# Gram and triangle products spread over eight tiles of the array, the triangle applied to the Gram side

## Chip, cores and metric

The kernel runs on one core of a Trainium2 chip. The metric is the device time of one execution in microseconds (us).

## What is computed

The input is a delta-rule attention over 4 batches of 8 heads, 768 positions and a head size of 48, followed by two feed-forward layers over the 3072 tokens. All inputs and outputs are float32 (the weights are wider on arrival and are decoded in the kernel). Cut to what matters:

```python
k_n = k / (np.linalg.norm(k, axis=-1, keepdims=True) + 1e-06)
state = np.zeros((B, H, D, D), dtype=np.float32)
for t in range(S):
    kt, vt, bt = (k_n[:, :, t], v[:, :, t], beta[:, :, t, None])
    y[:, :, t] = np.einsum('bhd,bhde->bhe', q[:, :, t], state)
    v_old = np.einsum('bhde,bhd->bhe', state, kt)
    state = state + bt[:, :, :, None] * np.einsum('bhd,bhe->bhde', kt, vt - v_old)
x = y.transpose(0, 2, 1, 3).reshape(B * S, H * D)
x = (silu(x @ w_gate) * (x @ w_val)) @ w_out      # 384 -> 1536 -> 384
out = elu(x @ w_in) @ w_out2                      # 384 -> 2048 -> 384
```

## The kernel before, in words

**Groups.** The recurrence is done in blocks of 32 positions. One group is 128 positions of 2 batches: 16 units (8 heads for each of the two batches, a = 0 and 1), each with C = 4 blocks of 32 positions, which lie at the partitions 0, 32, 64 and 96. There are 12 groups. A unit has the number u = 8 a + 2 j + par.

**Work of one group.** `loads` fetches k and q into `kp` and `qp`, and v into the right half of `R`. `prepare` normalises the keys, copies them into the left half of `R` (`rk`, L425, on ACT), writes beta times key into `gr` (`kb`, L430, on POOL), transposes keys and queries into `kq` (L441), and multiplies the blocks' keys with keys and queries (`gram`, L467: 32 rows of output, 64 columns, contraction over 48). `mask` (L473, on DVE) writes the strictly triangular parts of that, times beta, into `gr`. `invert` computes the inverse of the unit triangular 32x32 block of each unit on DVE: transposes into `ain` (L502), 31 elimination steps of a product and a sum (`whole`, L517 and L524), or, in groups 0, 1 and 2 (`BLOCKED`), 15 steps on the two halves at once (`halves`, L534 and L540), and a transpose back (L548); in the blocked groups a second transpose (L553) and two matmul steps (`join1`, L562, and `join2`, L576) put the halves together. The result is `zt`.

`attention` then applies the triangle: `xstep` (L618) multiplies `zt` with the 96 columns of `R`, four units to a step and four steps to a group, and `xput` (L622, on ACT) writes the result back into `R`. `gstep` (L638) multiplies `R` with the 80 columns of `gr`, and `put` (L647) evicts that into `lc`. `chain` (L671) carries the state over the blocks, `yall` (L694) makes the outputs, `xtr` (L718) transposes them for the feed-forward part.

**Feed-forward.** `moe1` (L853, L878) follows on each group: 12 times two projections of 9 matmuls and a product of 9. After the last group `moe2` (L963, L1000) runs over all tokens.

**Small matmuls.** Each step on 32 positions is a matmul that takes a part of the rows of the 128x128 array (the partitions of its operands) and a part of its columns (the partitions of its output). `gram` before uses 48 rows and four column groups, one unit parity after the other; `xstep` uses the four places on the diagonal, rows and columns 32 c. The trace has two records for each such matmul of the program, so 64 matmuls of a group are 128 records.

**Order.** The program writes its own order. Steps are handed to `Order.add` with an engine, an estimated duration, a priority, what they read and write, and how many PSUM banks they need (`Slots`; the pool AT has four). `Order.run` then lists the steps of each engine by estimated start and priority, so PE's order of attention and feed-forward work is fixed when the program is built. Where its plan has PE idle before 150 us, it puts filler matmuls (`fill`, L1030). Changed estimates change the order.

**Queues.** All loads and stores are issued on SP's queue in the planned order; the weight loads of the first feed-forward layer (L756, L759) follow the loads of group 0.

Of the kernel before, what the change touches and what calls it, by code (L numbers as in the profile page):

```python
# [17 lines left out]
ALU = mybir.AluOpType  # L18
# [162 lines left out]
def delta_moe_kernel(ctx: ExitStack, tc: tile.TileContext, q, k, v, beta,  # L181
                     wg, wv, wo, w_in, w_out, out):
    nc = tc.nc
# [9 lines left out]
    C = 4  # L193
# [175 lines left out]
    def loads(g, p, then=None):  # L369
# [12 lines left out]
    def prepare(g, p):  # L382
# [40 lines left out]
        def rk(a):  # L423
            u = slice(a * 8, a * 8 + 8)
            A.copy(out=R[:, u, 0:D], in_=kp[:, u, 0:D])  # L425
# [26 lines left out]
        for a in range(2):  # L452
            add(p, pool(384, lambda a=a: kb(a)), r=["nbt", "kp", ("kp", a)], w=[("grk", a)])
            add(p, act(384, lambda a=a: rk(a), False), r=["kp", ("kp", a)], w=[("Rk", a)])
        for a in range(2):
            l = []
            for par in range(2):
                h = Slots(AT, 1)

                def gram(a=a, par=par, h=h):  # L460
                    x = bank[h.got[0]][:, 0:256].rearrange("p (n w) -> p n w", n=4)
                    b = 64 * par
                    for j in range(4):
                        m = kq[b:b + D, a, j]
                        for c in range(C):
                            t = slice(32 * c, 32 * c + 32)
                            PE.matmul(x[t, j, :], lhsT=m[:, 1, t], rhs=m[:, :, t], start=True,  # L467
                                      stop=True, skip_group_check=True)

                def mask(a=a, par=par, h=h):  # L470
# [6 lines left out]

                def rest(a=a, par=par, h=h, mask=mask):
                    add(p, dve(256, mask), r=[h, "z"], w=[("grm", a, par)], use=[h])
                l.append((470, gram, [("kq", a, 0), ("kq", a, 1)], h, [("grm", a, par)], rest))  # L480
            batch(p, 6, l, g > 0)
# [4 lines left out]
    def invert(g, p):  # L486
# [18 lines left out]
        def whole(l):  # L505
            c0 = l // 2
            cuts = [(c0, 16)]
            if l * (16 - c0) > 40:
                cuts = [(c0, c0 + (16 - c0) // 2), (c0 + (16 - c0) // 2, 16)]
            b = 32 * (l + 1) % 1024  # L510
            ts = [ain[:, b + l * (x - c0):b + l * (y - c0)].rearrange("p (j n) -> p j n", n=y - x)
                  for x, y in cuts]
# [600 lines left out]
```

## Time and profile before

| | us |
|---|---|
| three runs | 1160.48, 1164.08, 1164.74 |
| median of the three | 1164.08 |
| profiled execution | 1164.54 |
| its span | 1162.80 |
| PE busy in the span | 1131.3 |
| DVE busy | 776.8 |
| ACT busy | 576.5 |
| POOL busy | 44.2 |

The span runs from the first to the last instruction of the program; 1.7 us of the execution lie around it. In the views, an engine is busy while one of its records runs; records of matmuls overlap, so many of them together take less time than their sum. "PEld" is the loading of weights, "xN" is a number of records, and PEclk is the share of the full TensorE clock that was granted in a stretch. "issue" as a releaser means that the profile shows nothing that the engine waited for.

### The profile page before, as it was taken

What the parts mean: (1) busy time and instruction counts of PE and PEld (TensorE: products, weight loads), DVE (VectorE), ACT (ScalarE), POOL (GpSimd) and SP (SyncE); (2) the same over time, 40 slices, a digit from 0 to 9 for tenths busy, and PEclk for the clock granted to TensorE, in tenths of its full rate; (3) what the DMA queues carried; (4) which work ended last, traced back from release to release, by engine and by line L of the source; (5) the groups of instructions that cost most, each with busy time, mean ns of one, the idle gap of its engine ahead of it and who ended that gap; (6) DMA issues with size and microseconds to landing.
All of it is one profiled execution on the core that took longest, in us unless ns stands there. A gap on an engine that the chain in (4) does not pass through costs nothing.

```text
span 1162.8 us, 34253 instructions
## 1 busy us (share of the span) xinstructions
PE 1131.3 (97%) x14766; PEld 1051.0 (90%) x14766; DVE 776.8 (67%) x2430; ACT 576.5 (50%) x1110; POOL 44.2 (4%) x61
## 2 busy tenths in 40 slices
PE   8889989999999999999999999999999999999998
PEld 7779889999999999899999999988889889888887
DVE  7789857877778786778786844996545444454444
ACT  8688433434343434243434344995545454454443
POOL 2000000000000000000000000000000000000000
PEclk9899899999999999899999999999999999999999
DMA  9650202020202020202020004900101001010000
GB/s 245 200 161 16 43 2 44 16 43 16 44 16 44 22 50 10 36 18 42 22 50 10 22 2 141 353 15 28 55 1 55 1 19 37 1 37 1 28 1 27
DMA packets 106822, 57.33 MB, mean 49 GB/s; under 512 B 76944, under 2 KB 101520, under 8 KB 106672
## 3 DMA queue, kind: packets, MB, share of 16 engines
q1 hardware_dynamic: 106672, 55.16, 17.5%
q8 instruction: 115, 1.88, 0.7%
q14 instruction: 35, 0.29, 0.1%
HBM read 45.71 MB, written 9.44 MB: 47 GB/s over the span
## 4 chain that ended last, share of the span: by engine, by line
PE 89%; DVE 5%; ACT 3%; issue 2%; DMA 0%; ACTq 0%; DVEq 0%
PE gv L853 27%; PE acc L878 12%; PE acc L1000 8%; PE at L1000 8%; PE at L963 8%; PE gv L963 8%; PE at L671 3%; PE at L638 3%; PE at L618 3%; PE at L441 2%; PE at L467 2%; PE at L694 1%; DVE z L540 1%; DVE ain L534 1%; PE at L718 1%
## 5 line engine op out<-in xcount | busy, mean ns | idle before, releaser
L853 PE MATMUL gv<-xh,w 128*128 128x256 f32 x1728 | 297.1, 291 | 1.0 <-ACT tb L860 0.9
L853 PEld LDWEIGHTS gv<-xh,w 128*128 128x128 f32 x1728 | 242.4, 193 | 9.1 <-ACT tb L860 1.4
L878 PE MATMUL acc<-hb,w 128*128 128x256 f32 x1296 | 182.3, 285 | 0.7 <-DVE hb L870 0.6
L878 PEld LDWEIGHTS acc<-hb,w 128*128 128x128 f32 x1296 | 165.9, 192 | 2.7 <-DVE hb L870 1.0
L860 ACT ACTIVATE tb<-gv 128x256 f32<-128x256 f32 x144 | 55.3, 384 | 200.3 <-PE gv L853 199.2
L853 PE MATMUL gv<-xl,w 128*128 128x256 f32 x864 | 151.7, 285 | 0.0
L853 PEld LDWEIGHTS gv<-xl,w 128*128 128x128 f32 x864 | 125.6, 194 | 0.0
L867 ACT CAST hb<-tb 128x256 fp32r<-128x256 f32 x144 | 58.5, 406 | 121.0 <-DVE tb L863 120.2
L863 DVE TENSOR_TENSOR tb<-gv,tb 128x256 f32<-128x256 f32 x144 | 60.7, 422 | 66.9 <-ACT tb L860 38.7
L978 DVE SCALAR_TENSOR_TENSOR hb<-gv,hb 128x512 f32<-128x512 f32 x48 | 33.2, 691 | 91.6 <-ACT hb L975 91.6
L524 DVE TENSOR_TENSOR z<-z,ain 128x60 f32<-128x60 f32 (+32 forms) x522 | 88.7, 209 | 0.9
L517 DVE TENSOR_TENSOR ain<-z,ain 128x60 f32<-128x60 f32 (+32 forms) x522 | 87.7, 204 | 0.6
L978 DVE SCALAR_TENSOR_TENSOR hb<-at,hb 128x512 f32<-128x512 f32 x48 | 33.1, 690 | 81.1 <-ACT hb L975 81.0
L870 DVE TENSOR_TENSOR hb<-tb,hb 128x256 fp32r<-128x256 f32 x144 | 66.3, 460 | 22.4 <-ACT hb L867 21.4
L969 ACT ACTIVATE hb<-gv 128x512 f32<-128x512 f32 x48 | 28.7, 597 | 96.7 <-PE gv L963 96.5
L975 ACT ACTIVATE hb<-hb,neg 128x512 f32<-128x512 f32 x96 | 69.5, 724 | 2.7
L969 ACT ACTIVATE hb<-at 128x512 f32<-128x512 f32 x48 | 28.7, 597 | 79.4 <-PE at L963 79.1
L972 ACT ACTIVATE hb<-hb 128x512 f32<-128x512 f32 x96 | 60.7, 633 | 2.8
L638 PE MATMUL at<-gr,R 32*96 32x80 f32 x1488 | 45.3, 251 | 0.0
L638 PEld LDWEIGHTS at<-gr,R 32*96 32x96 f32 x1488 | 37.7, 159 | 6.4
L1000 PE MATMUL acc<-w,ain 128*128 128x384 f32 x192 | 39.7, 340 | 1.8 <-DVE ain L983 1.2
L963 PE MATMUL gv<-lc,w 128*128 128x512 f32 x144 | 41.0, 394 | 0.0
(192 smaller groups left out, 2089.4 us busy)
## 6 DMA issues: line engine op xcount, KB each, us to landing
w<-in_moe_w_out_dram SPq DMA_DIRECT2D x28, 384.0 KB, 6.7
w<-in_moe_w_in_dram SPq DMA_DIRECT2D x16, 384.0 KB, 6.2
kp<-in_k_dram SPq DMA_DIRECT2D x12, 384.0 KB, 4.1
qp<-in_q_dram SPq DMA_DIRECT2D x12, 384.0 KB, 4.1
R<-in_v_dram SPq DMA_DIRECT2D x24, 192.0 KB, 2.8
w<-in_moe_w_gate_dram SPq DMA_DIRECT2D x12, 384.0 KB, 6.8
w<-in_moe_w_val_dram SPq DMA_DIRECT2D x12, 384.0 KB, 6.7
x2d<-hb SPq DMA_DIRECT2D x12, 256.0 KB, 2.0
```

What stands on the lines that cost most here:

```text
L517: V.tensor_tensor(out=t, in0=z[:, l:l + 1, x:y].to_broadcast([128, l, y - x]), in1=an[:, l, 0:l].unsqueeze(2).to_broadcast([128, l, y - x] ...
L524: V.tensor_tensor(out=z[:, 0:l, x:y], in0=z[:, 0:l, x:y], in1=t, op=ALU.add)
L638: PE.matmul(bank[h[c].got[0]][0:96, s * 80:s * 80 + 80], lhsT=R[t, u, :], rhs=gr[t, u, 0:80], start=True, stop=True, skip_group_check=True)
L853: PE.matmul(dst, lhsT=wt[:, a_, kk * 128:(kk + 1) * 128], rhs=xx[:, kk, :], start=(n == 0), stop=(n == 3 * KD - 1))
L863: V.tensor_tensor(out=c['s'], in0=bank[h.got[0]][:, TB:2 * TB], in1=c['s'], op=ALU.mult)
L870: return lambda: e.tensor_tensor(out=c['h'][:, 1, :], in0=c['s'], in1=c['h'][:, 0, :].bitcast(F32), op=ALU.subtract)
L878: PE.matmul(o_, lhsT=w[:, a_, d * 128:(d + 1) * 128], rhs=c['h'][:, b_, :], start=(f == 0 and n == 0 and d != 1), stop=(f == F1 - 1 and n ...
L963: PE.matmul(x, lhsT=W[f][:, 0, a_, kk * 128:(kk + 1) * 128], rhs=x2[n][b_][:, kk, :], start=(m == 0), stop=(m == 3 * KD - 1))
L972: A.activation(out=c['r'], in_=c['r'], func=ACTF.Exp, scale=-1.0)
L975: A.activation(out=c['r'], in_=c['r'], func=ACTF.Identity, bias=neg1, scale=1.0)
L978: V.scalar_tensor_tensor(out=c['r'], in0=bank[h.got[0]], scalar=0.0, in1=c['r'], op0=ALU.max, op1=ALU.add)
L1000: PE.matmul(o, lhsT=c['h'][:, b_, t * 128:(t + 1) * 128], rhs=W[f][:, 1][:, a_, :], start=(f == 0 and m == 0), stop=(f == F2 - 1 and m == 2))
```

## The change

**Gram.** The matmuls of both parities of one a go into one step, alternating: parity 0 uses the rows 0 to 47, parity 1 the rows 64 to 111, each with four column groups, and each parity writes its own PSUM bank. There are two Gram steps to a group in place of four.

**Triangle.** `xstep` multiplies `zt` with the 80 columns of `gr` in place of the 96 columns of `R`, and `xput` writes `gr` in place of `R`. Eight units go into one step and two banks: units 0 to 3 of an a use the diagonal, units 4 to 7 the places two column groups further. The results of the latter therefore come out shifted by two blocks of 32 positions. So that `gstep` finds both factors on the same partitions, `R` of these units is shifted in the same way: the copy of the keys and the load of v are cut into three pieces each (one for the unshifted units, one for each half of the shifted ones). `put` undoes the shift with its output pattern.

**Inversion.** As the triangle now stands on the other side, its transpose is needed: the elimination runs from the first position up in place of from the last down, with the same number and sizes of steps, reading columns of `an` in place of rows. In the blocked groups `join1` reads `zt` and `join2` reads the second transpose.

The diff, without the changed dependences of `load_x2`:

```diff
@@ loads
         for a in range(2):
-            add(p, dma(196608, lambda a=a: nc.sync.dma_start(
-                out=R[:, a * 8:a * 8 + 8, D:2 * D], in_=src_of(v, g, a, a + 1)), 160.0), w=[("Rv", a)])
+            def rv(a=a):
+                x = src_of(v, g, a, a + 1)
+                for u0, p0, p1, m0 in ((0, 0, 128, 0), (4, 0, 64, 64), (4, 64, 128, 0)):
+                    nc.sync.dma_start(out=R[p0:p1, a * 8 + u0:a * 8 + u0 + 4, D:2 * D],
+                                      in_=x[m0:m0 + p1 - p0, u0:u0 + 4])
+            add(p, [("SP", 1290.0, 0.0, 196608 / 160.0, rv)], w=[("Rv", a)])
@@ prepare
-            add(p, act(384, lambda a=a: rk(a), False), r=["kp", ("kp", a)], w=[("Rk", a)])
+            for n, c in enumerate(((0, 0, 128, 0), (4, 0, 64, 64), (4, 64, 128, 0))):
+                add(p, act(192, lambda a=a, c=c: rk(a, *c), False), r=["kp", ("kp", a)], w=[("Rk", a, n)])
         for a in range(2):
-            l = []
+            h = [Slots(AT, 1) for par in range(2)]
+
+            def gram(a=a, h=h):
+                for j in range(4):
+                    for c in range(C):
+                        for par in range(2):
+                            t = slice(32 * c, 32 * c + 32)
+                            m = kq[64 * par:64 * par + D, a, j]
+                            PE.matmul(bank[h[par].got[0]][t, 64 * j:64 * j + 64], lhsT=m[:, 1, t],
+                                      rhs=m[:, :, t], start=True, stop=True, skip_group_check=True)
+            add(p, pe(620, gram, 6), r=[("kq", a, 0), ("kq", a, 1)], w=h, need=h,
+                wait=[("grm", a, 0), ("grm", a, 1)])
...
-                l.append((470, gram, [("kq", a, 0), ("kq", a, 1)], h, [("grm", a, par)], rest))
-            batch(p, 6, l, g > 0)
@@ invert, whole
-                                    in1=an[:, l, 0:l].unsqueeze(2).to_broadcast([128, l, y - x]),
+                                    in1=an[:, l + 1:32, l:l + 1].to_broadcast([128, m, y - x]),
...
-        for l in range(15 if blocked else 31, 0, -1):
+        for l in range(15 if blocked else 31):
@@ invert, joins
-                    PE.matmul(x[r:r + 32, u], lhsT=gr[r:r + 16, u, 80:112], rhs=d1t[r:r + 16, u],
+                    PE.matmul(x[r:r + 32, u], lhsT=gr[r:r + 16, u, 80:112], rhs=zt[r:r + 16, u],
...
-                    PE.matmul(x[t, u], lhsT=buf['v'][t, u], rhs=zt[t, u], start=True, stop=True,
+                    PE.matmul(x[t, u], lhsT=d1t[t, u], rhs=buf['v'][t, u], start=True, stop=True,
...
-        add(p, pe(1250, join1, 8), r=GRM + ALLA[2:], w=[h1], need=[h1], wait=["z"])
+        add(p, pe(1250, join1, 8), r=GRM + ALLA[:2], w=[h1], need=[h1], wait=["z"])
-        add(p, pe(1250, join2, 8), r=["z"] + ALLA[:2], w=[h2], need=[h2])
+        add(p, pe(1250, join2, 8), r=["z"] + ALLA[2:], w=[h2], need=[h2], wait=ALLA[:2])
@@ attention
-        for n in range(4):
-            h = Slots(AT, 1)
+        for a in range(2):
+            h = [Slots(AT, 1) for n in range(2)]
...
-                        PE.matmul(x[t, j], lhsT=zt[t, 4 * n + j, :], rhs=R[t, 4 * n + j, :],
-                                  start=True, stop=True, skip_group_check=True)
+                    for n in range(2):
+                        u = a * 8 + 4 * n + j
+                        for c in range(C):
+                            t = slice(32 * c, 32 * c + 32)
+                            o = 32 * ((c + 2 * n) % C)
+                            PE.matmul(bank[h[n].got[0]][o:o + 32, 80 * j:80 * j + 80], lhsT=zt[t, u, :],
+                                      rhs=gr[t, u, 0:80], start=True, stop=True, skip_group_check=True)
...
-            add(p, pe(700, xstep, 7), r=ALLA[:2] + [("Rk", a), ("Rv", a)], w=[h], need=[h])
-            add(p, act(384, xput), r=[h], w=[("Rk", a), ("Rv", a)], use=[h])
+            add(p, pe(700, xstep, 7), r=ALLA[:2] + gk, w=h, need=h)
...
+                add(p, act(320, xput), r=[h[n]], w=gk, use=[h[n]])
...
-                            e(out=buf['lc', a][par][:, :, c, :], in_=pv)
+                            e(out=win(buf['lc', a][par][:, 0, c, 0:1],
+                                      [[640 + (160 if c < 2 else -160), 2], [320, 2], [1, 80]]), in_=pv)
```

## Rows read from the trace of the kernel before

**Rows 1.** The page's busy time of each engine: us, share, instructions.
```profile
PE 1131.3 (97%) x14766; PEld 1051.0 (90%) x14766; DVE 776.8 (67%) x2430; ACT 576.5 (50%) x1110; POOL 44.2 (4%) x61
```
**Rows 2.** The page's chain that ended last, shares of the span by line.
```profile
PE gv L853 27%; PE acc L878 12%; PE acc L1000 8%; PE at L1000 8%; PE at L963 8%; PE gv L963 8%; PE at L671 3%; PE at L638 3%; PE at L618 3%; PE at L441 2%; PE at L467 2%; PE at L694 1%; DVE z L540 1%; DVE ain L534 1%; PE at L718 1%
```
**Rows 3.** Busy us (count) by stretch: PE, PEld, DVE, ACT, POOL, PEclk, DMA, GB/s.
```profile
350.00:407.00 57.00, 56.92 (x1005) 54.31 (x1007) 44.13 (x190) 22.49 (x57) 3.24 (x4) 1.00 0.15 31
...
463.00:524.00 61.00, 59.23 (x995) 56.36 (x997) 44.32 (x189) 22.40 (x57) 3.23 (x4) 0.94 0.14 28
...
sum 513.00, PE 509.85 PEld 487.22 DVE 390.61 ACT 201.49 POOL 27.23; mean PE 56.65 PEld 54.14 DVE 43.40 ACT 22.39 POOL 3.02
```
**Rows 4.** The same view of the first 180 us.
```profile
0.00:90.00 90.00, 75.14 (x1526) 68.64 (x1527) 68.12 (x181) 70.50 (x93) 9.86 (x20) 0.94 0.73 196
90.00:130.00 40.00, 39.39 (x815) 36.06 (x814) 38.23 (x66) 31.68 (x60) 2.88 (x2) 1.00 0.12 22
130.00:180.00 50.00, 44.35 (x870) 41.76 (x867) 29.75 (x91) 17.19 (x42) 4.21 (x5) 0.90 0.08 20
```
**Rows 5.** PE's groups of instructions: shapes, count, busy us, mean ns, idle before.
```profile
L618 PE MATMUL at<-R,ain 32*32 32x96 f32 x1536 | 37.8, 253 | 2.2 <-issue 2.2
L1030 PE MATMUL acc<-identr 128*128 128x256 f32 x208 | 32.0, 306 | 4.0 <-ACT identr L1039 2.4 <-issue 1.5
L467 PE MATMUL at<-kq 48*32 48x64 f32 x1536 | 24.7, 228 | 3.4 <-issue 3.4
```
**Rows 6.** PE in order of time around two blocks: start us, us, what.
```profile
358.40 1.89 PE L467 MATMUL at<-kq 48*32 48x64 f32 x128
360.22 0.51 PE L853 MATMUL gv<-xh,w 128*128 128x256 f32 x2
...
390.75 2.84 PE L618 MATMUL at<-R,ain 32*32 32x96 f32 x128
393.52 0.63 PE L853 MATMUL gv<-xh,w 128*128 128x256 f32 x3
```
**Rows 7.** The same view around the first join of group 2.
```profile
155.07 1.28 PE L562 MATMUL at<-ain,gr 16*32 16x32 f32 x128 [0.94 <-DVE ain L553]
156.28 0.62 PE L853 MATMUL gv<-xh,w 128*128 128x256 f32 x3
```
**Rows 8.** Instructions of single lines: count, least/median/greatest ns, first and last start.
```profile
L553 DVE STREAM_TRANSPOSE ain<-ain x3: 674/689/711, 26.8 to 154.3; 128x512 f32<-128x512 f32 x3
...
L425 ACT COPY R<-kp x24: 502/512/531, 13.2 to 639.7; 128x384 f32<-128x384 f32 x24
...
L622 ACT COPY R<-at x48: 476/478/600, 39.6 to 679.6; 128x384 f32<-128x384 f32 x48
...
L647 ACT COPY lc<-at x92: 416/435/466, 45.3 to 689.4; 96x320 f32<-96x320 f32 x92
```
**Rows 9.** SP's queue at the start, in order of time.
```profile
2.73 0.41 SPq L374 DMA_DIRECT2D qp<-in_q_dram  x1
3.19 3.10 SPq L377 DMA_DIRECT2D R<-in_v_dram  x2
6.33 1.15 SPq L759 DMA_DIRECT2D w<-in_moe_w_gate_dram  x1
```
**Rows 10.** PE's waits in the first 180 us: us in total, times, longest.
```profile
PE at L576 <- issue: 4.8, 2, 4.0
```
**Rows 11.** PE's waits from 180 to 705 us.
```profile
PE at L467 <- issue: 1.7, 1, 1.7
PE at L671 <- issue: 0.8, 2, 0.6
```
**Rows 12.** The page's DMA queue of instructions: packets, MB, share.
```profile
q8 instruction: 115, 1.88, 0.7%
```
**Rows 13.** PE in order of time in group 8.
```profile
474.63 0.64 PE L467 MATMUL at<-kq 48*32 48x64 f32 x14 [1.70 <-issue]
```
**Rows 14.** Busy time by stretch after that wait.
```profile
473.00:481.00 8.00, 6.37 (x67) 5.89 (x67) 4.76 (x13) 0.38 (x1) 0.53 (x1) 0.57 0.02 3
```

More of the change, by code (lines that the diff above doesn't have):

```diff
@@ L421, in nkn, with rk @@
                             op=ALU.mult)
-        def rk(a):
-            u = slice(a * 8, a * 8 + 8)
-            A.copy(out=R[:, u, 0:D], in_=kp[:, u, 0:D])
+        def rk(a, u0, p0, p1, m0):
+            u = slice(a * 8 + u0, a * 8 + u0 + 4)
+            A.copy(out=R[p0:p1, u, 0:D], in_=kp[m0:m0 + p1 - p0, u, 0:D])
         def kb(a):
@@ L453, in prepare, with mask @@
             add(p, pool(384, lambda a=a: kb(a)), r=["nbt", "kp", ("kp", a)], w=[("grk", a)])
-            add(p, act(384, lambda a=a: rk(a), False), r=["kp", ("kp", a)], w=[("Rk", a)])
+            for n, c in enumerate(((0, 0, 128, 0), (4, 0, 64, 64), (4, 64, 128, 0))):
+                add(p, act(192, lambda a=a, c=c: rk(a, *c), False), r=["kp", ("kp", a)], w=[("Rk", a, n)])
         for a in range(2):
-            l = []
-            for par in range(2):
-                h = Slots(AT, 1)
[L460 to L470, printed above, removed]
+            h = [Slots(AT, 1) for par in range(2)]
[9 more added lines that the diff above has]
+                wait=[("grm", a, 0), ("grm", a, 1)])
+            for par in range(2):
+                def mask(a=a, par=par, h=h[par]):
                     x = bank[h.got[0]][:, 0:256].rearrange("p (n w) -> p n w", n=4)
@@ L476, in mask @@
                                     op=ALU.mult)
-                def rest(a=a, par=par, h=h, mask=mask):
-                    add(p, dve(256, mask), r=[h, "z"], w=[("grm", a, par)], use=[h])
-                l.append((470, gram, [("kq", a, 0), ("kq", a, 1)], h, [("grm", a, par)], rest))
-            batch(p, 6, l, g > 0)
+                add(p, dve(256, mask), r=[h[par], "z"], w=[("grm", a, par)], use=[h[par]])
         invert(g, p)
@@ L505, in whole @@
         def whole(l):
[L506 to L512, printed above, removed]
+            m, e = 31 - l, l // 2 + 1
+            cuts = [(0, e)]
+            if m * e > 40:
+                cuts = [(0, e // 2), (e // 2, e)]
+            ts = [ain[:, m * x:m * y].rearrange("p (j n) -> p j n", n=y - x) for x, y in cuts]
             def mul():
@@ L639, in gstep @@
                                       rhs=gr[t, u, 0:80], start=True, stop=True, skip_group_check=True)
[L640 removed]
+                add(p, pe(860, gstep, 3), r=[("Rk", a, 0), ("Rk", a, 1), ("Rk", a, 2), ("Rv", a), ("grk", a),
+                                              ("grm", a, par)],
                     w=h + ([] if par else lk[a]), need=h,
@@ L916, in load_x2 @@
               [(("sv", a, c), 1) for a in range(2) for c in range(C - 1)],
-              "R": [("Rk", 0), ("Rk", 1), ("Rv", 0), ("Rv", 1)],
+              "R": [("Rk", a, n) for a in range(2) for n in range(3)] + [("Rv", 0), ("Rv", 1)],
               "kq": [("kq", a, b) for a in range(2) for b in range(2)]}
```

37 lines of the change are left out of this document (16 added, 21 removed).

## Prediction, made before the change was run

> **What bounds the kernel now.** The busy line comes first: PE works for 97% of the span, DVE for 67%, ACT for 50% [rows 1]. Then the chain of waits: it is made of PE lines, the two MoE stages above all, and the two products that this change touches, L618 and L467, stand in it with 3% and 2% [rows 2]. A share of the whole span hides stages, so the third view is the table by stretch. From 180 to 693 us there are nine stretches of 56 to 57 us, one for each of groups 3 to 11; two of them and the sum of the nine stand in [rows 3]: PE is busy 509.85 of 513 us, DVE 390.61. One stretch is odd, 61 us with a granted clock of 0.94; I come back to it. There PE is the bound, and PE time taken away is span taken away. The first 180 us are another matter [rows 4]: PE is busy 75.14 of the first 90 us, but 32.0 us of PE's work in the run are filler matmuls, L1030 [rows 5], which the program puts only where its plan has PE idle, so PE does not bound there; from 90 to 130 us it does (39.39 of 40), from 130 to 180 us in part (44.35 of 50). After 693 us no touched PE work is left.
>
> **The change part by part.** *The two products.* Each of 12 groups runs 128 Gram records and 128 triangle records (1536 of each [rows 5]; the trace has two records for one matmul of the program). In group 6 the Gram block starts at 358.40 and the next PE work at 360.22: 1.82 us all in. The triangle block starts at 390.75, the next at 393.52: 2.77 us [rows 6]. The records last 228 and 253 ns but follow each other after 13 to 20 ns, so the array holds several at once: four, since the code spreads each over four tiles of the array. Both blocks have the same count, and 64 against 96 columns: 32 columns are worth 0.95 us. By that line 128 records of 32 columns would take 1.82 - 0.95 = 0.87 us. The trace has such a block, the join at L562: 155.07 to 156.28, 1.21 us [rows 7]. So under some 1.2 us for 128 records the columns no longer count; something that goes by the record does.
>
> With eight in flight the Gram block would take half of 1.82, 0.91 us, by columns, and 1.21 by records; I take 1.21, the measured row. The triangle goes from 96 to 80 columns (2.77 - 0.47 = 2.30 us) and then to half, 1.15 us; both limits lie close together there, so I take 1.30. Saved per group: 0.61 + 1.47 = 2.08 us. The other ends: nothing gained by eight (1.82 and 2.30 us, 0.47 saved) and no floor (0.91 and 1.15 us, 2.53 saved). Nine groups lie in the PE-bound stretch: 9 x 2.08 = 18.7 us. Groups 1 and 2 lie ahead of 180 us; 4.2 us of PE time goes there, and I count 2.0, between none and all, since PE binds only from 90 us and not throughout. Group 0 counts nothing, its time was filler.
>
> One row speaks to whether two products that share rows of the array overlap: in the Gram block before, all four use the same 48 rows of kq and differ in columns alone, and they run at 13 ns each. The Trainium skill, "TensorE: Matmul & The Clock Gate", Part 3, "The mechanism", says a weight load overlaps running matmuls only when their row group differs; this block contradicts that as a general rule. By the rule the new triangle, two to a row group, would gain only its columns (rival B).
>
> *The inversion* runs the other way round with the same 15 or 31 steps of the same sizes, reading columns of `an` in place of rows. No row shows such a pattern; a tenth more or less on these steps would leave DVE, busy 43 of 57 us a group [rows 3], as unbound as it is, so nothing is taken. In the three blocked groups the second transpose, L553 (689 ns [rows 8]), leaves the path ahead of the first join and lies beside it; join 2 waits for it, behind 1.2 us of join 1. Only group 0 can feel that: 0.7 us.
>
> *Waits.* Both products now need two PSUM banks at once. Before, a group's four triangle steps took the pool's four banks one after the other in one unbroken block [rows 6], and so do two steps with two each; MoE matmuls stand behind them on PE. The triangle step no longer waits for R; it waits for gr, which is complete before the inversion starts. The Gram side is evicted by the same four ACT copies, and gstep waits for them as before. Nothing is counted; if a bank comes late, PE stands for one eviction, 0.4 us a group.
>
> *ACT.* The copy of the keys, L425 (512 ns, 24 of them), becomes three of half the columns. From 384 to 320 columns an eviction fell from 478 (L622) to 435 ns (L647) [rows 8], 0.67 ns a column, so a half copy is about 383 ns, three are 1.15 us, 0.64 more, 1.3 us a group. The four evictions of the triangle lose 43 ns each. ACT gains some 1.1 us of work a group, where it is busy about 22.5 of 57 us [rows 3]: hidden, as is the eviction at L647, whose strides alone change. If the cover fails, at the start (ACT 70.5 of 90 us [rows 4]), the price is up to 1.1 us.
>
> *DMA.* Each load of v becomes three, 48 more issues in all on SP's queue. Behind them in the queue stand the weight loads, and for them ACT and DVE wait. At the start two issues took 3.10 us and the first weight load went out at 6.33 us [rows 9]; if time goes by bytes nothing is added, if by issue 4 x 1.55 = 6.2 us. The keys and queries, twice the bytes each, were issued in about 0.4 us, so I take 1.0. Later the queue is idle. Start in all: -0.7 (transpose), -1.0 (group 0's shorter blocks on the way to its first MoE stage), +1.0 (DMA), +0.7 (ACT): zero, with some 3 us either way.
>
> *A wait that grows.* Some PE idle time is put down to "issue", with no engine late: 4.8 us at L576 [rows 10] and 2.2 at L618 [rows 5], 1.7 and 0.8 us at L467 and L671 after 180 us [rows 11], each time in or right behind blocks of short matmuls. The queue marked "instruction" moved 115 packets and 1.88 MB [rows 12]; over 2 x 14766 PE records [rows 1] that is 64 bytes a record and 256 records a packet, a whole Gram block with its weight loads. So a short block eats one packet's worth, and the next one can be late; in group 8 it was, in the middle of a Gram block [rows 13]. That made its stretch 61 us against 56.5: 4.5 us, of which 1.7 are the wait and the rest is the clock, 0.57 of full over the next 8 us, half speed for most of it [rows 14]. A faster block asks for the next packet sooner and comes up to 2.08 us earlier to the point where it needs it. Bounds: nothing, or all of the 18.7 us given back. The nearest rows are the 2.5 us that the nine groups wait already; I take 4.0 us more, and one more fall of the clock, 2.8 us.
>
> The Trainium skill, "Runtime: NRT & Kernel Launch", section "Instruction fetch mechanics", has the same blocks of 256 instructions and calls crossing them mostly hidden. By that the sum would be 1143.8 us; the 2.5 us above disagree.
>
> **Sum.** 18.7 + 2.0 - 0.0 - 4.0 - 2.8 = 13.9 us. The profiled execution took 1164.54 us, span 1162.8; the median of the three runs is 1164.08, so it is a typical one. 1164.5 - 13.9 = 1150.6: I say 1151.
>
> **Rivals.**
> A, the sum above. For it: PE is full in nine groups and the blocks are short and separate. Range 1140 (no floor, no more late packets: 9 x 2.53 + 2.0 = 24.8) to 1158 (late packets return another 7).
>
> B, the change does not do what it says: eight do not run at once, because two to a row group exclude each other or because the engine does not look far enough ahead in its queue to find the other tiles' work. Then only the columns count: 9 x 0.47 = 4.2 us, 1160. Against it stands the Gram block before; nothing in the trace shows eight.
>
> C, late packets take the gain back: every one of nine groups waits about 1.3 us longer, 11.7 us, and the clock falls once more: 1164.5 - 20.7 + 11.7 + 2.8 = 1158 to 1161. For it: every block of 128 is a packet. Against it: join 1, at 1.21 us, ran through without a wait.
>
> D, slower: the late packet is long enough in most groups to bring the clock down. A wait of 0.6 us (the longest at L671) left it up, 1.7 us took it down. At 4.5 us a group this pays for the 20.7 us from the fifth group on; with six, 1164.5 - 20.7 + 27 = 1171. The place is the triangle block, which loses most of its length.
>
> **How the numbers follow.** A 0.70, B 0.11, C 0.10, D 0.09. The likeliest is A, 1151. The range 1140 to 1162 takes in A, B and C and leaves out D and a little under A. A measurement here can tell about 0.5% (5.8 us) from no change. Faster by more than that means under 1158.3: nearly all of A (0.68) and some of B and C (0.06), 0.74. Within it: the rest of B and C, 0.17. Slower: D, 0.09.
>
> **What would show it.** Right: the Gram block at 1.2 us and the triangle block at 1.3 us all in; groups at 54 to 55 us; PE still full from 180 to 690 us; "issue" waits of 5 to 8 us there. B: the blocks at 1.8 and 2.3 us. C and D: "issue" rows at the triangle line in most groups, without and with a granted clock under 1 in those stretches. Wrong in another way: DVE or ACT named as releaser of PE in the nine stretches, or the first MoE matmul later than before at the start.

## The result: a little slower

The changed kernel takes 1171.89 us (median of 6 runs, 1168.45 to 1172.79), the kernel before 1164.21 beside it (1160.48 to 1164.92): 1.007 of the time, 95% interval 1.0051 to 1.0089. The forecast was 1151, the range 1140 to 1162, so both missed. The profiled execution took 1171.76 us, span 1170.1.

The busy line and the instruction queue on the page of after:

```profile
PE 1121.1 (96%) x14794; PEld 1037.7 (89%) x14794; DVE 778.3 (67%) x2432; ACT 584.1 (50%) x1156; POOL 44.3 (4%) x61
q8 instruction: 116, 1.90, 0.7%
```

PE works 10.2 us less than in [rows 1], yet the span is 7.3 us longer: PE stands idle for 49.0 us in place of 31.5. Where, the table by stretch says (columns as in [rows 3]):

```profile
0.00:90.00 90.00, 72.33 (x1496) 66.15 (x1497) 63.65 (x176) 65.91 (x91) 9.79 (x20) 0.88 0.73 196
90.00:130.00 40.00, 36.77 (x733) 34.19 (x735) 35.02 (x54) 32.70 (x59) 3.04 (x2) 0.98 0.13 22
130.00:180.00 50.00, 47.37 (x1013) 44.61 (x1005) 36.61 (x110) 21.20 (x52) 3.35 (x4) 0.97 0.08 19
180.00:693.00 513.00, 495.77 (x8788) 470.82 (x8782) 390.40 (x1678) 203.34 (x533) 28.08 (x35) 0.99 0.15 29
```

Against [rows 3, 4], PE is idle 14.1 us more from 180 to 693 us (17.2 for 3.15) and 2.4 us more before that; the last 1.0 us come after 693. What PE waited for from 180 to 705 us (us in total, times, longest):

```profile
PE at L695 <- issue: 4.2, 4, 1.9
PE at L469 <- issue: 2.9, 3, 1.4
PE at L617 <- DVE ain L545: 2.8, 7, 0.6
PE gv L854 <- ACT xh L725: 1.7, 4, 1.1
PE gv L854 <- DVE xl L729: 1.6, 3, 1.1
PE at L637 <- issue: 1.3, 2, 0.9
PE gv L854 <- issue: 1.2, 1, 1.2
PE acc L879 <- issue: 0.5, 1, 0.5
PE at L445 <- ACT dt L647: 0.4, 1, 0.4
```

In [rows 11] there were two such lines, 2.5 us. Now "issue" makes 10.1 us, at yall (L695), Gram (L469) and elsewhere, and a new kind has come: 6.5 us in which PE waits for DVE or ACT, nearly all of it at the triangle (L617, for the transpose back, L545) and at the first MoE piece of a group (L854, for the two parts xh and xl of its input). A MoE piece is here nine matmuls of the feed-forward part.

The blocks themselves became shorter. PE in order of time around the triangle block of group 6, and around the two Gram halves of group 8:

```profile
401.01 1.60 PE L617 MATMUL at<-gr,ain 32*32 32x80 f32 x128
402.55 0.39 PE L854 MATMUL gv<-xh,w 128*128 128x256 f32 x1
...
483.07 0.86 PE L469 MATMUL at<-kq 48*32 48x64 f32 x64
483.86 0.62 PE L854 MATMUL gv<-xh,w 128*128 128x256 f32 x3
...
485.98 0.71 PE L469 MATMUL at<-kq 48*32 48x64 f32 x46
487.59 0.38 PE L469 MATMUL at<-kq 48*32 48x64 f32 x18 [0.91 <-issue]
```

The triangle takes 1.54 us for the 2.77 of [rows 6]. Gram takes twice 0.79 us for 1.82, in two halves that stand apart, with a MoE piece and a chain step between them; the second half here meets an "issue" wait; without it the halves take 0.79 us each. Saved per group: 1.23 + 0.24 = 1.47 us.

So the balance of the profiled runs is: blocks, 12 x 1.47 = -17.6; idle, +17.5; filler matmuls, +5.4 (37.4 us of them for 32.0); one clock fall behind 719.6 us, +1.7 (3.4 us at a granted clock of 0.50). Together +7.0, where the span grew by 7.3. This is a sum and names no causes: filler stands where the plan has PE idle before 150 us, so more of it means more planned idle time there.

### The profile page after: what moved, and what is told of

Read it like the earlier page. It is cut to its first block, busy times and chain, and to the rows that moved or that the text cites. A ratio compares the mean times of both kernels' runs of the same rounds, so it can differ in the third digit from the quotient of the medians.

```text
span 1170.1 us, 34493 instructions
## 1 busy us (share of the span) xinstructions
PE 1121.1 (96%) x14794; PEld 1037.7 (89%) x14794; DVE 778.3 (67%) x2432; ACT 584.1 (50%) x1156; POOL 44.3 (4%) x61
## 4 chain that ended last, share of the span: by engine, by line
PE 79%; DVE 12%; ACT 5%; issue 3%; DMA 0%; POOLq 0%; DVEq 0%; ACTq 0%
PE gv L854 25%; PE acc L879 11%; PE acc L1001 8%; PE gv L964 8%; PE at L1001 8%; PE at L964 7%; PE at L637 3%; PE at L672 2%; PE at L617 2%; PE at L445 2%; PE at L469 1%; DVE ain L502 1%; PE at L695 1%; DVE sv L678 1%; DVE ain L545 1%
## 5 line engine op out<-in xcount | busy, mean ns | idle before, releaser
L854 PE MATMUL gv<-xh,w 128*128 128x256 f32 x1728 | 295.7, 290 | 6.6 <-ACT xh L725 2.9
L854 PEld LDWEIGHTS gv<-xh,w 128*128 128x128 f32 x1728 | 243.2, 194 | 12.5 <-ACT xh L725 3.8
L854 PE MATMUL gv<-xl,w 128*128 128x256 f32 x864 | 153.1, 286 | 2.3 <-DVE xl L729 2.3
L854 PEld LDWEIGHTS gv<-xl,w 128*128 128x128 f32 x864 | 125.7, 194 | 3.6 <-DVE xl L729 3.5
L864 DVE TENSOR_TENSOR tb<-gv,tb 128x256 f32<-128x256 f32 x144 | 60.6, 421 | 83.1 <-PE gv L854 44.1
L871 DVE TENSOR_TENSOR hb<-tb,hb 128x256 fp32r<-128x256 f32 x144 | 62.1, 431 | 19.9 <-ACT hb L868 18.3
L1031 PE MATMUL acc<-identr 128*128 128x256 f32 x236 | 37.4, 312 | 4.0 <-ACT identr L1040 2.4
```

The source lines that it names most:

```text
L854: PE.matmul(dst, lhsT=wt[:, a_, kk * 128:(kk + 1) * 128], rhs=xx[:, kk, :], start=(n == 0), stop=(n == 3 * KD - 1))
L864: V.tensor_tensor(out=c['s'], in0=bank[h.got[0]][:, TB:2 * TB], in1=c['s'], op=ALU.mult)
L871: return lambda: e.tensor_tensor(out=c['h'][:, 1, :], in0=c['s'], in1=c['h'][:, 0, :].bitcast(F32), op=ALU.subtract)
```

## Experiments

Names with b_ are the kernel before with an edit, with a_ the changed kernel with an edit, with a4_ the changed kernel with the old Gram code and an edit. Times are medians; the ratio is that to the kernel before measured beside it, with its 95% interval. "Issue" and "DVE, ACT" are PE's waits from 180 to 705 us in the profiled execution, in us. That is one execution, and it can lie some us off the median: it took 1171.0 us for a_tick, 1161.0 for b_cuts, 1181.0 for a_gramj and 1144.0 for b_moe_less.

| kernel | us | ratio | issue | DVE, ACT |
|---|---|---|---|---|
| before | 1164.2 | 1 | 2.5 | 0 |
| after | 1171.9 | 1.0070 (1.0051 to 1.0089) | 10.1 | 6.5 |
| b_moe_less | 1147.8 | 0.9875 (0.983 to 0.992) | 3.4 | 2.9 |
| b_elim_less | 1164.7 | 1.0010 (0.9989 to 1.003) | 3.9 | 0 |
| a_elim_less | 1170.2 | 1.0064 (1.004 to 1.0087) | 9.7 | 6.0 |
| b_gram8 | 1167.3 | 1.0042 (1.0023 to 1.0061) | 7.3 | 5.5 |
| a_gram4 | 1165.0 | 1.0011 (0.9995 to 1.0028) | 9.2 | 0.7 |
| a_est | 1169.5 | 1.0056 (1.0029 to 1.0083) | 10.6 | 2.8 |
| a_gramj | 1185.4 | 1.0189 (1.0157 to 1.022) | 17.6 | 1.3 |
| b_cuts | 1167.2 | 1.0034 (1.0009 to 1.0058) | 3.6 | 0 |
| a_tick | 1165.1 | 1.0022 (1.0004 to 1.0039) | 4.2 | 10.5 |
| a4_tick | 1164.2 | 1.0008 (0.9989 to 1.0027) | 9.9 | 0 |
| a_vlate | 1168.5 | 1.0050 (1.0028 to 1.0073) | 9.7 | 6.4 |
| a4_tick_vlate | 1160.1 | 0.9981 (0.9965 to 0.9996) | 9.9 | 0 |
| a_gramw | 1163.5 | 1.0004 (0.9988 to 1.002) | 3.1 | 8.3 |
| a_tick_lat | 1161.4 | 0.9987 (0.9967 to 1.0007) | 5.8 | 8.5 |
| a_etv | 1166.0 | 1.0047 (1.0027 to 1.0067) | 8.4 | 6.0 |
| a_etvl | 1166.3 | 1.0039 (1.0018 to 1.0059) | 4.7 | 8.9 |
| a_tlv | 1159.8 | 0.9966 (0.9950 to 0.9982) | 6.0 | 9.1 |
| a_tlv25 | 1163.1 | 0.9990 (0.9973 to 1.0007) | 5.3 | 8.6 |

### Is PE the bound, or the attention's chain through DVE?

The first theory after the result was that one group's attention (Gram, elimination on DVE, triangle, next group) had been as long as PE's work all along. Three runs speak on it.

b_moe_less:

```diff
+                    cut = 2 <= g <= 10 and (j == 1 or f % 2 == 0)
...
+                            if cut and n == 3 * KD - 1:
+                                continue
...
-                                      start=(n == 0), stop=(n == 3 * KD - 1))
+                                      start=(n == 0), stop=(n == 3 * KD - 1 - cut))
```

> The kernel before with 18 MoE matmuls fewer in each of the groups 2 to 10 (the last matmul of 18 of 24 projections; their contribution is left out of the sums), every step in its old place in the order: some 1.9 us of PE time a group, about as much as the change takes from Gram and triangle, but from work that is not on the attention's own chain. If PE time is the bound, as the prediction has it, 9 x 1.9 = 17 us: 1147. If the chain of one group's attention (Gram, mask, elimination on DVE, triangle, and round to the next group) is already as long as the 57 us of PE's work, PE only waits more: 1160 to 1164.

b_elim_less; a_elim_less has the same with `10 <= l <= 19`, the steps of the same sizes:

```diff
+            if not blocked and 12 <= l <= 21:
+                mul = acc_ = lambda: None
```

> The kernel before with 10 of the 31 elimination steps left out in the groups 3 to 11 (40 DVE instructions of some 0.22 us, 8.7 us a group), every step left in its old place. PE is full there, so by either theory the gain is small: at most the 3 us of PE idle time from 180 to 693 us, 1160 to 1164.

> The changed kernel with the same 10 elimination steps left out in the groups 3 to 11. If the attention's chain through DVE is what PE now waits for, PE fills up again: of its 17 us idle from 180 to 693 us some 10 to 14 go, and the wait of the last group's MoE with them: 1155 to 1162. If late instruction packets are the cause, nothing of that depends on DVE: 1169 to 1174, with 'issue' rows as long as they are now.

More than the expected 17 us of PE work went: the busy time of the cut matmuls' group (xh) fell from 297.1 to 276.2 us, by 20.9. Of that, 15.5 us came back in the medians (interval 9 to 20) and 20.6 between the profiled executions: PE was the bound, and the chain theory, which gave 0 to 4, falls on that. It falls a second time on a_elim_less, which gained 1.7 us, within the intervals. Its busy times from 180 to 693 us and its wait at the triangle:

```profile
180.00:693.00 513.00, 496.45 (x8779) 471.59 (x8777) 342.70 (x1320) 203.91 (x534) 27.55 (x35) 0.99 0.15 29
```

```profile
PE at L619 <- DVE ain L547: 2.8, 7, 0.6
```

DVE works 48 us less in these stretches, and PE waits for its transpose exactly as long as before. So that wait is not set by the amount of DVE's work in the steps left out. The trace of after shows what stands between them and the wait, DVE and PE in order of time around one of the seven:

```profile
458.62 0.42 DVE L864 TENSOR_TENSOR tb<-gv,tb 128x256 f32<-128x256 f32 x1
...
459.37 1.12 DVE L545 STREAM_TRANSPOSE ain<-z 128x512 f32<-128x512 f32 x1
...
460.63 0.49 PE L617 MATMUL at<-gr,ain 32*32 32x80 f32 x29 [0.37 <-DVE ain L545]
```

Ahead of the last elimination steps DVE's order has a MoE product (L864) that needs, by way of ACT, a PE piece just done; then follow the steps and the transpose, and PE, whose own order has the triangle right there, comes 0.4 us too early. In six of the seven L864 itself waits there for ACT (0.13 to 0.19 us). Taking DVE work out ahead of L864 cannot move that.

### Which part of the change brings the waits?

b_gram8 puts the Gram code of the change into the kernel before; a_gram4 puts the old Gram code into the changed kernel (the diff of `prepare` shown above, forward and back). a_est:

```diff
-            add(p, pe(620, gram, 6), r=[("kq", a, 0), ("kq", a, 1)], w=h, need=h,
+            add(p, pe(940, gram, 6), r=[("kq", a, 0), ("kq", a, 1)], w=h, need=h,
...
-            add(p, pe(700, xstep, 7), r=ALLA[:2] + gk, w=h, need=h)
+            add(p, pe(1400, xstep, 7), r=ALLA[:2] + gk, w=h, need=h)
```

> The kernel before with the Gram change alone (two steps of two banks, both parities alternating). By the prediction's sum 9 x 0.25 us (two blocks of 0.79 against one of 1.82): 1162. If the chain theory holds, the two halves with MoE work between them make the chain some 1.9 us a group longer and save next to nothing: 1166 to 1178. If late packets are the cause: within 3 us of 1164, since a half block is no denser than a triangle block.

> The changed kernel with the Gram products of the kernel before (four steps of one bank, one parity each); triangle, shift and inversion stay changed. If what the Gram steps of two banks do to the order is the cause (halves apart, PE waiting for DVE and ACT at the triangle and at the first MoE piece of a group), these waits go and the 1.2 us a group of the triangle come through: 1150 to 1156. If late instruction packets behind any faster block are the cause, the triangle at 1.53 us is enough for them: 'issue' rows of 7 us or more from 180 to 705 us, 1160 to 1168.

> The changed kernel with one thing different: the order is made with the durations that the kernel before gave to the same work (940 in place of 620 for a Gram step, 1400 in place of 700 for a triangle step of two banks), so the work on the chip is the same and only its order may change. If the estimates made the order worse, 5 us or more come back: 1160 to 1167. If the need for two banks or the packets are the cause: 1169 to 1174.

The Gram change alone makes the kernel before slower, by 0.42%, and brings the same picture of waits, with the old triangle:

```profile
PE at L689 <- issue: 4.8, 5, 1.4
PE at L613 <- DVE ain L543: 2.4, 7, 0.5
PE gv L848 <- DVE xl L723: 1.6, 2, 0.9
PE at L464 <- issue: 1.6, 2, 1.3
PE gv L848 <- ACT xh L719: 1.5, 3, 1.1
```

The 1167.3 us of b_gram8 also lie in the range that its text gave for the chain theory, so that run alone would not have refuted it. Without the Gram change (a_gram4) the waits for DVE and ACT are gone but for 0.7 us; from 200 us on PE's order is that of the kernel before. But the triangle's 9 x 1.23 = 11 us still don't come through: "issue" is at 9.2 us. Both readings written down for that run were half right. The old durations in the plan (a_est) take the waits for DVE and ACT from 6.5 to 2.8 us; "issue" stays, and 2.4 us of gain is less than the 5 expected, so 1169.5 lies in the other reading's range.

### Are the "issue" waits late instruction packets?

a_gramj makes the two Gram steps of a group one step that takes four banks:

```diff
-            add(p, pe(620, gram, 6), r=[("kq", a, 0), ("kq", a, 1)], w=h, need=h,
-                wait=[("grm", a, 0), ("grm", a, 1)])
+            gs.append(gram)
+        add(p, pe(1240, lambda: [f() for f in gs], 6), r=[("kq", a, b) for a in range(2) for b in range(2)],
+            w=gh[0] + gh[1], need=gh[0] + gh[1], wait=GRM)
```

> The changed kernel with the two Gram steps of a group as one step that takes four banks, so that its 128 records run in one block as in the kernel before. If the split into two halves with MoE pieces between them is the cause, this takes it away: 1154 to 1162. If packets are the cause, a block of 128 records in 1.57 us asks for them faster than the two halves: 'issue' at the Gram line in several groups, 1170 to 1180. If it has to wait for four free banks, PE shows that as a wait at the Gram line.

It is 1.9% slower, beyond the ranges of both readings, with PE's order now chain, yall, chain, xtr and Gram without a MoE piece between them. A wait in yall, and the stretch behind it:

```profile
312.63 0.24 PE L700 MATMUL at<-sv,l 96*32 96x48 f32 x1 [3.69 <-issue]
```

```profile
312.60:320.00 7.40, 7.37 (x191) 6.46 (x191) 4.71 (x12) 1.44 (x3) 0.53 (x1) 0.50 0.02 6
```

That is 3.7 us of waiting and 7.4 us at a granted clock of 0.50, the lower of the two levels.

a_gramw has the same steps in the same order and the same columns, with half the matmuls for Gram (its results are not the products):

```diff
-                for j in range(4):
+                for j in (0, 2):
...
-                            PE.matmul(bank[h[par].got[0]][t, 64 * j:64 * j + 64], lhsT=m[:, 1, t],
-                                      rhs=m[:, :, t], start=True, stop=True, skip_group_check=True)
+                            x = bank[h[par].got[0]][t, 64 * j:64 * j + 128].rearrange("p (n w) -> p n w", n=4)
+                            PE.matmul(x, lhsT=m[:, 1, t], rhs=kq[64 * par:64 * par + D, a, j:j + 2].rearrange(
+                                "p n k t -> p (n k) t")[:, :, t], start=True, stop=True, skip_group_check=True)
```

> The changed kernel with half as many Gram matmuls, each of twice the columns (the products of every second unit are left out, and the other half of each result is of no use); every step in its old place, the same number of columns through the array. It tells two things. If the block's length goes by columns, a half takes about the 0.79 us that it took; if it goes by the record, about 0.4 us. And PE has 128 instructions of 256 less to fetch for the Gram products of a group: if late instruction packets are the cause of the 'issue' waits, these fall from 10 us to 6 or less from 180 to 705 us, and the time to 1163 to 1168; if their cause is another, they stay and so does the time, 1169 to 1173.

Its "issue" waits from 180 to 705 us, and a Gram half in order of time:

```profile
PE gv L855 <- issue: 1.0, 1, 1.0
PE at L696 <- issue: 0.9, 3, 0.5
PE acc L880 <- issue: 0.8, 1, 0.8
PE at L638 <- issue: 0.4, 1, 0.4
```

```profile
305.34 0.67 PE L470 MATMUL at<-kq 48*32 48x128 f32 x32
305.94 0.62 PE L855 MATMUL gv<-xh,w 128*128 128x256 f32 x3
```

With 128 instructions a group less, the "issue" waits fall from 10.1 to 3.1 us and the time by 8.4 us, of which the shorter block explains 9 x 0.38 = 3.4. The waits for DVE and ACT stay (8.3 us for 6.5). A half takes 0.60 us: between the two readings, so neither columns nor records alone set it. With half the records it lost 0.19 of 0.79 us.

a_tick changes no step, only the order. A planned delay of 4 us, on an engine that does not exist, writes `yt`, which yall then reads; this holds yall back, and five MoE pieces stand ahead of it in place of one. The steps behind it shift with it:

```diff
+        if 1 <= g < NB - 1:
+            add(p, [("TK", 1.0, 4000.0, 0, lambda: None)],
+                r=[x for a in range(2) for x in (("sv", a, C - 2), (("sv", a, C - 2), 1))], w=["yt"])
         batch(p, 5, [yall(0), yall(1)], g > 0)
```

> The changed kernel with the output step yall (groups 1 to 10) held back in the order until some 4 us after the last state update that it reads, so that five MoE pieces in place of one stand between the second Gram half and yall; the same work, no instruction more. If late instruction packets in the dense run chain, Gram, chain, Gram, yall cost the time, the 4.2 us of 'issue' at yall and one fall of the clock go: 1162 to 1167. If 'issue' there is not the packets, the waits stay about as long wherever yall stands: 1170 to 1174.

> The changed kernel with the Gram products of the kernel before, and yall held back in the same way (five MoE pieces in place of two ahead of it). It has next to no waits for DVE and ACT, so the packets alone should stand between it and the triangle's gain of 9 x 1.24 us: with 'issue' down from 9 us to 3 or less, 1154 to 1160. If the packets are late behind the triangle and Gram blocks themselves, whatever follows: 1163 to 1167.

In a_tick the 4.2 us at yall are gone, and its median is 6.8 us under that of after. Its profiled execution, the longest of its ten, does not show that gain: it took 1171.0 us for 1171.8, with 1.9 us less of waits in all. So the lines below show that the waits at yall went, not where the 6.8 us came from. All its PE waits from 180 to 705 us:

```profile
PE at L617 <- DVE ain L545: 4.7, 9, 0.6
PE at L469 <- issue: 4.0, 5, 1.2
PE gv L857 <- DVE xl L729: 3.5, 8, 0.4
PE gv L857 <- ACT xh L725: 2.3, 7, 1.1
PE at L637 <- issue: 0.2, 1, 0.2
```

In a4_tick the same edit did not help: "issue" is 9.9 us, at Gram and the blocks behind it. There Gram is one block again, right behind a chain step, and yall was not where the packets were late. The second reading held.

So the count of instructions close together matters, and the traces show the packet itself. Count PE's records, matmuls and weight loads, from the start of the run: when the "issue" waits over 0.45 us of after from 20 to 720 us ended, all 16 of them, PE stood 193 to 195 records past 256 times the number of packets that had landed. The same holds for all 251 such waits of the 20 kernels, while PE's waits for DVE and ACT stand at any count. So these waits come at one place of a packet alone, where PE has run what had arrived and needs the next one. PE's 1.43 us wait at Gram in after ended at 428.61. The stretches around it, by the columns of [rows 3], with the share of the DMA engines and GB/s at the end (a share over 1 means that the times of packets overlap); then what the instruction queue moved from 425.65 to 427.10, and all DMA from 427.10 to 428.60:

```profile
424.00:425.65 1.65, 1.65 (x72) 1.56 (x67) 1.56 (x5) 0.00 (x0) 0.00 (x0) 1.00 1.46 164
425.65:427.10 1.45, 1.45 (x56) 1.18 (x55) 0.65 (x3) 0.38 (x1) 0.00 (x0) 1.00 0.14 22
427.10:428.60 1.50, 0.08 (x7) 0.00 (x0) 0.87 (x3) 0.00 (x0) 0.00 (x0) 1.00 0.00 0
428.60:432.60 4.00, 3.99 (x120) 3.68 (x124) 2.60 (x7) 0.41 (x1) 0.53 (x1) 0.61 0.01 4
```

```profile
q8 instruction: 1, 0.02, 6.1%
...
DMA packets 0, 0.00 MB, mean 0 GB/s; under 512 B 0, under 2 KB 0, under 8 KB 0
```

One packet moved, right behind loads for the next group at 164 GB/s, and PE ran dry until some 1.5 us after it had landed; then the clock fell. Read in this way, all "issue" waits over 0.45 us from 180 to 705 us in before (2), after (10) and a_gramj (8) ended 2.3 to 3.0 us after a packet of that queue began to move. Both of before, and seven of the eight of a_gramj, had data loads in the 3 us ahead of the packet; of the ten of after only three had, all at Gram, and none of those at yall. So data loads are not needed for a wait, and no run tests what they add.

### The start, and the waits that the order makes

b_cuts cuts the copies and the loads in the kernel before (the loads are shown):

```diff
-            add(p, dma(196608, lambda a=a: nc.sync.dma_start(
-                out=R[:, a * 8:a * 8 + 8, D:2 * D], in_=src_of(v, g, a, a + 1)), 160.0), w=[("Rv", a)])
+            def rv(a=a):
+                x = src_of(v, g, a, a + 1)
+                for u0, p0, p1 in ((0, 0, 128), (4, 0, 64), (4, 64, 128)):
+                    nc.sync.dma_start(out=R[p0:p1, a * 8 + u0:a * 8 + u0 + 4, D:2 * D],
+                                      in_=x[p0:p1, u0:u0 + 4])
+            add(p, dma(196608, rv, 160.0), w=[("Rv", a)])
```

a_vlate moves group 0's loads of v behind the first weights, and a4_tick_vlate does it on a4_tick:

```diff
-            add(p, [("SP", 1290.0, 0.0, 196608 / 160.0, rv)], w=[("Rv", a)])
+            add(p if g else 4.5, [("SP", 1290.0, 0.0, 196608 / 160.0, rv)], w=[("Rv", a)])
```

> The kernel before with each copy of the keys and each load of v cut into the three pieces of the change, written to their old places, and in the old order. By the prediction 1.0 us from the loads and up to 0.7 us from the copies at the start: 1164 to 1166. If the 3 us by which the changed kernel is late at the first MoE piece are theirs: 1167.

> The changed kernel with the six v loads of group 0 behind the first four pairs of weight loads on SP's queue. If the cut loads delay the first weights and cost the 3 us by which the first MoE piece is late: 1167 to 1170. If that delay is not theirs: 1171 to 1174.

> The last two edits together on the changed kernel with the old Gram products. Both gains add up if the causes are apart: 2 to 4 us under the one without the late v loads, 1150 to 1158.

SP's queue in after, in b_cuts and in a_vlate:

```profile
3.19 5.43 SPq L380 DMA_DIRECT2D R<-in_v_dram  x6
8.66 0.60 SPq L760 DMA_DIRECT2D w<-in_moe_w_gate_dram  x1
```

```profile
8.68 0.60 SPq L764 DMA_DIRECT2D w<-in_moe_w_gate_dram  x1
```

```profile
3.12 2.10 SPq L760 DMA_DIRECT2D w<-in_moe_w_gate_dram  x1
```

The first weights go out 2.33 us later than in [rows 9], and the first MoE piece of the run starts at 70.3 us in after, at 67.1 in before, at 67.3 in a_vlate. Two things make these numbers less plain than they look.

First, the late weights alone do not delay that piece. b_cuts sends them as late as after does and starts the piece at 67.1, as before does. a_elim_less, a_gramw and a_tick have PE's order of after up to there and its loads, and start it at 70.9 to 71.7; a_vlate, in the same order with the loads moved, at 67.3. So in after's order the place of the loads is worth some 3 us at the start, and in the order of before it is worth nothing there; what in the order makes the difference stays open. In the medians, moving the loads gave 3.4 us on the changed kernel (the intervals overlap), 4.1 us on a4_tick and 1.6 us on a_tick_lat (a_tlv, below). b_cuts also lost 3.4 us in the median, with a profiled execution 6 us shorter than that: where that loss lies stays open.

Second, the first MoE piece does not stand at the same place in the two orders. PE in order of time in before, and then in after:

```profile
67.07 0.62 PE L853 MATMUL gv<-xh,w 128*128 128x256 f32 x3
...
70.34 0.72 PE L467 MATMUL at<-kq 48*32 48x64 f32 x30 [1.70 <-issue]
70.99 1.01 PE L853 MATMUL gv<-xh,w 128*128 128x256 f32 x3
```

```profile
69.94 0.45 PE L469 MATMUL at<-kq 48*32 48x64 f32 x12 [0.29 <-issue]
70.33 1.01 PE L854 MATMUL gv<-xh,w 128*128 128x256 f32 x3
```

In before the first piece runs ahead of the last quarter of group 1's Gram block and of the wait in it; in after it stands behind all of Gram. The second piece, behind all of Gram in both, starts at 70.99 and at 72.41 us: after is 1.4 us late there, not 3.2.

a_tick_lat is a_tick with longer planned ends for two DVE steps:

```diff
-        add(p, [("DVE", 1000.0, 1090.0, 0, back)], r=["z"], w=ALLA)
+        add(p, [("DVE", 1000.0, 1690.0, 0, back)], r=["z"], w=ALLA)
...
-                add(p, dve(384, lo), r=[h, ("xh", g % 2, a)], w=[("xl", g % 2, a)], use=[h])
+                add(p, [(e, o_, l_ + 600.0, k_, f_) for e, o_, l_, k_, f_ in dve(384, lo)],
+                    r=[h, ("xh", g % 2, a)], w=[("xl", g % 2, a)], use=[h])
```

> The changed kernel with yall held back as before, and with the order made as if the transpose back on DVE and the copy of the low part xl each took 0.6 us longer to end. If the waits of PE for DVE and ACT (10.5 us from 180 to 705 us with yall held back) come from an order that puts PE's next step a little too early, they go, and 4 to 8 us with them: 1157 to 1161. If DVE itself is too late, PE waits as long as before behind other MoE pieces: 1164 to 1167.

The 4.7 us at the triangle went entirely: they were the order's. The waits for xh and xl rose from 5.8 to 8.5 us. The time fell by 3.7 us, less than expected.

The last four join the edits: a_etv is a_est, a_tick and a_vlate together, a_etvl adds the longer ends, a_tlv is a_tick_lat with a_vlate, and a_tlv25 holds yall back by 2500 in place of 4000.

> Three edits on the changed kernel together: the old durations in the plan (940 and 1400), yall held back, and the v loads of group 0 behind the first weights. With the 7.1 us of 'issue' at yall gone, one fall of the clock with them, and 3.4 us for the loads, 1169.5 becomes 1156 to 1160; with the packets late elsewhere instead, 1161 to 1166.

> The same three edits and the 0.6 us longer ends of the transpose back and of xl in the plan. If the waits for DVE and ACT are the order's, these go too: 1153 to 1158. If not: within 2 us of the kernel without this edit.

> The changed kernel with yall held back some 4 us, the longer planned ends of the transpose back and of xl, and the v loads of group 0 behind the first weights. If the cures add, 3.4 us less than without the late v loads: 1156 to 1160, faster than both kernels; if not, 1161 to 1164.

> The same with yall held back 2.5 us in place of 4, which leaves two MoE pieces ahead of it and puts it earlier, so that the first MoE piece of a group waits less for xh and xl (8.5 us from 180 to 705 us with 4). If the packets keep up with two pieces, 1154 to 1158; if 'issue' at yall comes back, 1160 to 1166.

a_tlv is faster than both kernels, by 0.34% against the kernel before, as its text had it, with a gain of 1.6 us for the late loads in place of 3.4. a_etv and a_etvl are not: in their orders "issue" turned up at Gram and at the triangle, in chain steps or in MoE pieces. Holding yall back less (a_tlv25) left the waits for xh and xl nearly as they were (8.2 us for 9.1) and cost 3 us, so neither reading's cause was shown: these waits are not the price of the longer hold, and what they come from stays open.

## Why the prediction was wrong

The largest part of the miss is a term that the sum put at nothing, the waits for DVE and ACT that a new order brings (6.5 us); behind it come the size of the two blocks (5.5), the late packets (3.6 more than counted) and the time ahead of 180 us. The prediction's own sign of being wrong in another way, DVE or ACT as releaser of PE in the nine stretches, is what came.

**What bounds the kernel: right.** b_moe_less took 20.9 us of PE work away and got 15.5 us in the median.

**The two products: the mechanism right, the size off.** Eight at a time run, against rival B: the triangle is far under the 2.30 us that columns alone give. But 1.58 and 1.54 us stand in place of 1.21 and 1.30, so nine groups saved 9 x 1.47 = 13.2 us, not 18.7. The step that failed is the floor, "under some 1.2 us the columns no longer count": that 1.21 us was read from the join, a block on four places with 32 columns, and carried over to eight. On eight, 64 and 80 columns cost nearly the same, but 12 ns a record in place of 9.5, and at 128 columns (a_gramw) a record costs 19 ns, so there columns count as well.

**Waits: "nothing is counted" was wrong, 6.5 us.** The argument looked at banks, and of after's waits only one can be for a bank (0.4 us at the transposes, L445, behind an eviction, L647). What it passed over is that changed steps and durations make the program write another order: Gram came apart in halves, and PE's next step was put 0.4 us ahead of a transpose or of xh and xl. a_gram4 ties these waits to the Gram step, a_elim_less shows that they are not DVE's load, a_tick_lat that the one at the triangle goes with the plan.

**Late packets: the mechanism right, the size off.** 7.6 us more "issue" in place of 4.0. The place was wrong as well: in the nine stretches not in the triangle block, but in the run of chain, Gram and yall; ahead of 180 us the triangle did wait (3.5 us for 2.2 before). The Trainium skill, "Runtime: NRT & Kernel Launch", section "Instruction fetch mechanics", calls crossing a block of 256 instructions mostly hidden. In before that nearly held (2.5 us in 180 to 705 us); with a_gramj it cost 17.6.

**The clock.** One fall more, 2.8 us, was counted in the nine stretches. Before had one there of 6.8 us, after has two of 3.4, at half speed each: no more in sum. The third fall of after, 1.7 us, lies behind them. Ahead of 180 us the granted clock of after was lower on the whole (0.88 for 0.94 in the first 90 us); PE is not full there, and no run shows what that cost.

**Start: counted zero.** The first MoE matmul came 3.2 us later than before, the sign that the prediction named, but compared behind the same work it is 1.4 us, inside the 3 us either way. The price of the cut loads on the queue lay between "by bytes" and "by issue"; 2.33 us came, not 1.0.

**Groups 1 and 2** were to give 2.0 us. Of the blocks' 4.4 us in groups 0 to 2 nothing can be seen: ahead of 180 us PE was idle for 2.4 us more, and the 5.4 us of added filler lies there.

**Costed rightly:** the inversion (elimination products 208 ns for 204, sums 209 for 209), the copies of the keys (3 x 351 ns, 1.05 for 1.15 us), the triangle's eviction (429 for 435 ns).

**Rivals.** C named the late packets but had no other loss beside them. D's 1171 us is the measured time by chance: it has the clock fall in six of the nine groups, and it fell in two. a_gramj shows D's mechanism more strongly, with "issue" waits of up to 3.7 us and a granted clock of 0.97 from 180 to 693 us.

**What stays open.** The terms above do not add up to the whole: of the 7.3 us by which the span grew, 0.9 come from the nine stretches (14.1 us more idle time for 13.2 of shorter blocks), 1.7 from the clock fall at 719.6 us and 1.0 from idle time behind 693 us. The other 3.7 us have no place; moving the loads is worth about as much (3.4 us in a_vlate), but only in that order.

## What to carry to other kernels

Where a program writes its own order, a faster step is also a new order: compare the sequence of steps on each engine before and after, and price the places where one engine's next step now stands right behind another's. Short matmuls cost instructions as well as array time: where several blocks of them follow one another, put long matmuls between them, or use fewer and wider ones. Cutting one load in three at the head of a queue sent what stands behind it out 2.33 us later; whether that costs time depended here on PE's order, and moving the load behind what is needed first gained 1.6 to 4.1 us in the three kernels where it was tried.

## What the hardware showed that was not expected

The same steps in another order took 1165.1 us (a_tick) or 1171.9 (after): 0.6% by holding one step back in ten groups.

Matmuls of 64 columns on eight places of the array start every 12.3 ns on average (0.79 us for 64 records), those of 80 columns every 12.0 ns (1.54 us for 128); before, on four places, it was 14.2 and, with 96 columns, 21.6 ns [rows 6]. The step from four to eight places took 13% off the Gram products; off the triangle it took, with the 16 columns less, 44%.

Every long "issue" wait stands at the same place of a packet of 256 records, in all 20 kernels (above): the trace can tell a late packet from any other wait by counting.

The clock went to its lower level for 3.4 us after an "issue" wait of 1.4 us at Gram (429.5 to 432.9 us), and for 7.4 us and more after one of 3.7 us (a_gramj).
